# Other places for attention steps, splits and fill matmuls in the periods of a packed-attention and gated-FFN kernel

## The chip, the core and the metric

The kernel runs on one core of a Trainium2 chip. The metric is the device time of one execution in microseconds (us), as the median of the runs. The engines are PE (TensorE: matmuls and transposes), DVE (VectorE), ACT (ScalarE), POOL (GpSimd) and SP (which issues the DMAs).

## The reference, cut to what matters

Eight batches, 8 heads, 576 tokens, head dimension 64, 32 packing queries; then a gated feed-forward layer of 1536 columns over all 4608 tokens. Everything is float32.

```python
def sm_attn(qq, kk, vv):
    s = scale * np.matmul(qq, kk.transpose(0, 1, 3, 2))
    a = np.exp(s - np.max(s, axis=-1, keepdims=True))
    a = a / (np.sum(a, axis=-1, keepdims=True) + 1e-09)
    return np.matmul(a, vv)

p_packed = sm_attn(p, k, v)
x = sm_attn(q, p_packed, p_packed)          # then heads and dims as 512 columns
out = ((x @ w_a) * (x @ w_b)) @ w_out
```

## The kernel before, in words

**The two products of the FFN.** x is never formed. The second attention's weights a2 (transposed, 256 rows by 576 tokens per batch) are multiplied with g = packed values times w_a and w_b. Each float32 factor is split into a rounded part `hi` and a remainder `lo`, and a product is three matmuls: hi·hi, hi·lo, lo·hi. h, the gated product, is split in the same way and multiplied with w_out; this second product is called the fill, since its matmuls (512 columns, L726) are put between those of the first.

**The late part.** Batches 0 and 1 are done by an earlier part of the program. The change and the prediction are about batches 2 to 7, done in 72 periods (`period`, from L816), n = 0 to 71, twelve to a batch; two lead-in periods, -2 and -1, come ahead of them. Period n finishes column block n of h and starts block n + 1, with seven products of 288 columns (`product`, L767):

- products 5 (block n) and 1 (block n + 1) write PSUM bank pair X, product 2 writes V; ACT copies X to `d` (L834);
- first fill; DVE adds V to `d` (L839);
- products 3 and 6 add to X; ACT copies X's half to `c2` (L848); DVE multiplies X by `d` into one half of `hf` (tile name `asb`, L853);
- second fill; products 4 and 7 add to V; DVE adds `c2` to V (L865) and multiplies into the other half of `hf` (L866);
- third fill.

PE must wait where a product writes a bank that another engine still reads: product 3 for the `d` copy, product 4 for the `d` add, product 2 of the next period for the second `hf` multiply. How much PE has to do in between is set by the three fill counts.

**Beside that.** Every second period begins with `make_g` (L781 and after): PE forms g for two blocks, ACT and DVE take it apart, and POOL forms the combinations `gs` (L796). `split_g` (ACT cast `G_hi` at L802, then POOL remainder `G_lo` at L91) and `split_h` (ACT cast `h_hi` at L812, then POOL `h_lo` at L91) make the split factors; `hf` has two buffers. The attention of the batch ahead is cut into steps: `S` and `r` (first attention), `s` (second attention), `L` (loads on SP), `k`, `q`, `T`, `P` (turning of operands), `t` (`half_sums`: four POOL subtractions, L604) and `u0` to `u3` (`half_parts`: ACT casts L618, then remainders on DVE at L91). A u step makes the tiles `a_hi`, `a_lo`, `tx_hi`, `tx_lo` that the next batch's products read.

**What sets the order.** Engines work their queues in the order in which the program is written, and this order is written by hand: the table `STEPS` says which step comes at which point of a period (`pre`, `post`, `a`, `b`, `c`, `end`), one entry for each of the 12 periods of a batch; `FILLS` holds the three fill counts of an even and an odd period, for pairs of periods with 2 and with 3 tiles (24 and 36 matmuls). The places of `split_g` and `split_h` are fixed in `period`: `split_h(n - 1)` ahead of product 3, `split_g` after the `d` copy in odd periods and after the `c2` copy in even ones.

Of the kernel before, what the change touches and what calls it, by code (L numbers as in the profile page):

```python
# [19 lines left out]
def tile_packed_attn_gated_ffn(  # L20
# [483 lines left out]
    SUBS = ("0100")  # L504

    PLAN = (" |  |  | S0 | r0 | r0 |  | r0 |  | r0 Lv1 ; S1 | r1 | r1 q0 Lk2 | r1 | r1 | q1 Lk3 Lv2 P0 |  ; s0 | s0 s0 | s0 T2 | "
            "s0 Lp4 | s0 s1 | s1 s1 | s1 | s1 | s1 | t u0 | k2 |  | k3 Lq2")
    PLAN = dict(enumerate(PLAN.split("|")))
    PLAN_0 = ("A | C C | B A B A | B C C B C | A A | C | B | C B A T0 k0 Lp2 A | A A B B C Lq0 | C C k1 | A B A | "
# [88 lines left out]

    late = {}

    def half_sums(b):

        x0, x1, tf = a2f_of[b, 0], a2f_of[b, 1], late["tf"]
        sub = lambda out, a, c: nc.gpsimd.tensor_tensor(out=out, in0=a, in1=c, op=ALU.subtract)  # L604
        sub(tf[:, 1], x1[:, 1], x0[:, 1])
        sub(x0[:, 1], x0[:, 1], x0[:, 0])
        sub(tf[:, 0], x1[:, 1], x0[:, 1])
        sub(tf[:, 2], x1[:, 0], tf[:, 0])

    def half_parts(b, n):  # L610

# [10 lines left out]
    def emit_steps(b, steps):  # L622

        for name in steps.split():
            if name in "ABCD":
                emit(0, name)
            elif b >= B:
                continue
            elif name == "t":
                half_sums(b)  # L630
# [184 lines left out]
    def period(n, fills, steps):  # L815

        X, V = banks_of["x"], banks_of["v"]
        here, there, more = 0 <= n < LAST, 0 <= n + 1 < LAST, n + 2 < LAST
        k0, k1 = n % 2, (n + 1) % 2
        b = NB + n // NFT  # L820
        both = slice(0 if here and k0 == 0 or there and k1 == 0 else 1, 2 if here and k0 == 1 or there and k1 == 1 else 1)
        step = lambda at: emit_steps(b + 1, steps.get(at, ""))
        step("pre")
        if more and n % 2 == 0:
            make_g(n + 2)
        step("post")
        if here:
            product(n, 5, X, False)
        if there:
            product(n + 1, 1, X, True)  # L830
            product(n + 1, 2, V, True)
        if here or there:
            d = d_of[n] = lp.tile([P, 2, HS], F32, name="d", bufs=2)
            nc.scalar.copy(out=d[:, both], in_=X[:, both, 0:HS])  # L834
        if more and n % 2:
            split_g(n + 2)
        fill(fills[0])
        if here or there:
            nc.vector.tensor_tensor(out=d[:, both], in0=V[:, both, 0:HS], in1=d[:, both], op=ALU.add)  # L839
        flush()  # L840
        step("a")
        split_h(n - 1)
        if here:
            product(n, 3, X, False)
        if there:
            product(n + 1, 6, X, False)
            c2 = c2_of[n + 1] = lp.tile([P, HS], F32, name="c2", bufs=2)
            nc.scalar.copy(out=c2, in_=X[:, k1, 0:HS])  # L848
        if more and n % 2 == 0:
            split_g(n + 2)  # L850
        if here:
            hf = hf_of[n] = sm.tile([P, 2, HS], F32, name="asb")
            nc.vector.tensor_tensor(out=hf[:, 1], in0=X[:, k0, 0:HS], in1=d[:, k0], op=ALU.mult)  # L853
        step("b")
        fill(fills[1])
        flush()
        step("c")
        if here:
            product(n, 4, V, False)
        if there:  # L860
            product(n + 1, 7, V, True)
        if here:
            c2 = c2_of.pop(n)
            v = V[:, k0, 0:HS]
            nc.vector.tensor_tensor(out=v, in0=v, in1=c2, op=ALU.add)  # L865
            nc.vector.tensor_tensor(out=hf[:, 0], in0=v, in1=d_of.pop(n - 1)[:, k0], op=ALU.mult)  # L866
# [13 lines left out]
    while slot[0] <= max(plan) or (slot[0] - start) % 4:  # L880
        fill(6)
        flush()
        between()
    STEPS = {-2: {"post": "u1", "a": "u2", "c": "u3"}, 0: {"pre": "S0", "c": "Lq1", "end": "r0 Lv1"}, 1: {"a": "r0", "b": "r0 r0"},
# [5 lines left out]
    banks_of["x"], banks_of["v"] = bank_pair(), bank_pair()  # L890
    FILLS = {2: ((5, 3, 4), (6, 6, 0)), 3: ((7, 5, 6), (9, 9, 0))}
    for n in (-2, -1):
        period(n, (12, 12, 12), STEPS.get(n, {}))
    fill(99)
    flush()
    for n in range(LAST):
        b, ft = NB + n // NFT, n % NFT
        if ft % 2 == 0:
# [4 lines left out]
        period(n, FILLS[len(some)][ft % 2], STEPS[ft])  # L903
    split_h(LAST - 1)
    fill(99)
    flush()
# [45 lines left out]
```

## Time and profile before

| | |
|---|---|
| median of 3 runs | 718.42 us (718.34 to 718.44) |
| the profiled execution | 717.8 us, span 716.0 us |
| PE busy | 699.4 us, 98% |
| DVE, ACT, POOL busy | 444.8, 360.8, 419.2 us |
| chain that ended last | PE 89%, DVE 4%, POOL 3% |
| DMA | 102.37 MB, mean 143 GB/s |

The span is the time from the first to the last instruction of the profiled execution. A row of a timeline gives start, length, engine, line, operation, out<-in and, in square brackets, idle time of the engine before it and what ended that. Ends of matmuls are modelled, so a PE that waits is read from the starts of its matmuls rather than from its busy share.

### The profile page before, as it was taken

To read this page: it belongs to the slowest core of one execution; us is meant where nothing else is said; L and a number is where in the kernel's file an instruction comes from. 1 tells how busy PE (TensorE), PEld (TensorE's weight loads), DVE (VectorE), ACT (ScalarE), POOL (GpSimd) and SP (SyncE) were. 2 spreads that over 40 slices of the span, in tenths; PEclk is the share of its full clock that TensorE was granted. 3 is DMA by queue.
4 is the path that set the end of the run, shared out by engine and by line. 5 is a ranking of instruction groups with operands and counts; after the bars stand their busy time and mean duration, and the time that the engine had idled before them with its cause. 6 is when DMAs were issued, how large, how long until landed. Compare 5 with 4: busy or idle time off the path is not lost.

```text
span 716.0 us, 14183 instructions
## 1 busy us (share of the span) xinstructions
PE 699.4 (98%) x5558; PEld 574.3 (80%) x5558; DVE 444.8 (62%) x819; ACT 360.8 (50%) x733; POOL 419.2 (59%) x322
## 2 busy tenths in 40 slices
PE   6899999999999999999999999999999999999998
PEld 4488878888878887888888887788788878788887
DVE  3888655467355677665875677665685657654342
ACT  3788744544344555445554456454554445544520
POOL 0595743337245678565875488565776477756520
PEclk9999999999999999999999999999999999999999
DMA  8999863677354725545443563456245323123002
GB/s 256 386 259 307 236 135 72 175 170 272 82 127 149 189 77 149 142 123 148 145 97 122 141 187 92 109 177 165 71 112 165 110 83 119 60 103 133 1 1 74
DMA packets 177059, 102.37 MB, mean 143 GB/s; under 512 B 141280, under 2 KB 159456, under 8 KB 171616
## 3 DMA queue, kind: packets, MB, share of 16 engines
q1 hardware_dynamic: 176992, 101.47, 49.9%
q8 instruction: 43, 0.70, 0.4%
q14 instruction: 24, 0.20, 0.1%
HBM read 85.72 MB, written 15.73 MB: 142 GB/s over the span
## 4 chain that ended last, share of the span: by engine, by line
PE 89%; DVE 4%; POOL 3%; SPq 1%; DMA 1%; ACT 1%; issue 1%; DVEq 0%; POOLq 0%; ACTq 0%
PE x L726 35%; PE m L767 27%; PE m L389 9%; PE m L415 5%; PE x L781 4%; PE s L301 2%; PE s L316 1%; PE s L255 1%; POOL tf L604 1%; PE x L371 1%; DVE tx_lo L91 1%; PE s L291 1%; SPq L116 1%; POOL h_lo L91 1%; DMA kn<-in_k_dram 1%
## 5 line engine op out<-in xcount | busy, mean ns | idle before, releaser
L726 PE MATMUL x<-wo,h_hi 128*128 128x512 f32 (+1 forms) x776 | 242.1, 392 | 0.0
L91 POOL TENSOR_TENSOR h_lo<-asb,h_hi 128x576 fp32r<-128x576 f32 x96 | 139.2, 1450 | 52.5 <-ACT h_hi L408 37.1
L726 PEld LDWEIGHTS x<-wo,h_hi 128*128 128x128 f32 x776 | 138.0, 188 | 20.0 <-ACT gs L787 0.9
L726 PE MATMUL x<-wo,h_lo 128*128 128x512 f32 (+1 forms) x388 | 151.9, 391 | 0.0
L91 POOL TENSOR_TENSOR G_lo<-gs,G_hi 128x640 fp32r<-128x640 f32 x72 | 115.6, 1609 | 53.2 <-ACT G_hi L802 51.1
L91 POOL TENSOR_TENSOR A_lo<-gs,A_hi 128x256 fp32r<-128x256 f32 x36 | 26.8, 744 | 107.0 <-ACT A_hi L790 107.0
L726 PEld LDWEIGHTS x<-wo,h_lo 128*128 128x128 f32 x388 | 72.9, 188 | 13.5
L853 DVE TENSOR_TENSOR asb<-m,d 128x288 f32<-128x288 f32 x72 | 32.7, 455 | 78.0 <-ACT c L848 77.5
L834 ACT COPY d<-m 128x576 f32<-128x576 f32 (+1 forms) x73 | 46.7, 640 | 57.4 <-PE m L767 56.1
L736 DVE TENSOR_TENSOR part<-x,part 128x512 f32<-128x512 f32 (+1 forms) x65 | 44.4, 682 | 37.4 <-PE x L726 37.4
L787 ACT COPY gs<-x 128x512 f32<-128x512 f32 x36 | 21.2, 588 | 89.6 <-PE x L781 89.6
L767 PE MATMUL m<-tx_lo,G_hi 128*128 128x288 f32 x216 | 63.6, 295 | 2.6 <-DVE tx_lo L91 2.6
L839 DVE TENSOR_TENSOR d<-m,d 128x576 f32<-128x576 f32 (+1 forms) x73 | 54.0, 740 | 19.0 <-ACT d L834 18.7
L767 PE MATMUL m<-tx_hi,G_hi 128*128 128x288 f32 x216 | 64.2, 297 | 0.0
L767 PE MATMUL m<-tx_hi,G_lo 128*128 128x288 f32 x216 | 63.7, 295 | 0.0
L802 ACT CAST G_hi<-gs 128x640 fp32r<-128x640 f32 x72 | 52.6, 731 | 14.8 <-POOL gs L796 14.8
L848 ACT COPY c<-m 128x288 f32<-128x288 f32 x72 | 28.9, 402 | 57.4 <-PE m L767 57.4
L767 PEld LDWEIGHTS m<-a_hi,G_hi 128*128 128x128 f32 x144 | 27.0, 187 | 34.6 <-issue 17.4
L812 ACT CAST h_hi<-asb 128x576 fp32r<-128x576 f32 x72 | 49.1, 682 | 5.2 <-DVE asb L866 5.2
L865 DVE TENSOR_TENSOR m<-m,c 128x288 f32<-128x288 f32 x72 | 33.3, 462 | 24.0 <-PE m L767 22.1
L767 PE MATMUL m<-a_hi,G_hi 128*128 128x288 f32 x144 | 46.5, 323 | 1.4 <-ACT d L834 1.4
L796 POOL TENSOR_TENSOR gs<-gs 128x512 f32<-128x512 f32 x36 | 46.8, 1299 | 0.0
(171 smaller groups left out, 1550.7 us busy)
## 6 DMA issues: line engine op xcount, KB each, us to landing
wr<-w_kept SPq DMA_DIRECT2D x36, 1024.0 KB
nat<-in_k_dram SPq DMA_DIRECT2D x56, 144.0 KB
nat<-in_q_dram SPq DMA_DIRECT2D x56, 144.0 KB
vt<-in_v_dram SPq DMA_DIRECT2D x28, 256.0 KB
out_dram<-part SPq DMA_DIRECT2D x27, 256.0 KB
raw<-in_moe_w_a_dram SPq DMA_DIRECT2D x12, 512.0 KB
raw<-in_moe_w_b_dram SPq DMA_DIRECT2D x12, 512.0 KB
raw<-in_moe_w_out_dram SPq DMA_DIRECT2D x12, 512.0 KB
```

The costliest lines, as they stand in the source:

```text
L91: return eng.tensor_tensor(out=dst, in0=src, in1=hi.bitcast(F32), op=ALU.subtract)
L389: nc.tensor.matmul(out=ps[:, half, 0:HS], lhsT=gt[:, kt, ft % 4, cols], rhs=at[:, kt, HS * half:HS * half + HS], start=(n == 0 and kt == 0 ...
L415: nc.tensor.matmul(out=o[:, cols], lhsT=ht[:, c0:c0 + P], rhs=wt[:, cols], start=(ft == 0 and n == 0), stop=(ft == NFT - 1 and n == 2))
L726: nc.tensor.matmul(out=o[:, cols], lhsT=ht[:, c0:c0 + P], rhs=wt[:, cols], start=(ft == fts[0] and n == 0), stop=end)
L736: nc.vector.tensor_tensor(out=parts[i][:, cols], in0=o[:, cols], in1=parts[i][:, cols], op=ALU.add)
L767: nc.tensor.matmul(out=bank[:, n % 2, 0:HS], lhsT=g, rhs=t, start=(first and i == 0), stop=(i == 2), skip_group_check=True)
L796: nc.gpsimd.tensor_tensor(out=gs[:, 2:4].rearrange("p a u f -> p a (u f)"), in0=gs[:, 0:2].rearrange("p a u f -> p a (u f)"), in1=s2.unsqu ...
L802: nc.scalar.copy(out=G_hi[:, n % 3], in_=gs[:, 1:6, n % 2])
L812: nc.scalar.copy(out=view(h_hi[ft]), in_=src)
L834: nc.scalar.copy(out=d[:, both], in_=X[:, both, 0:HS])
L839: nc.vector.tensor_tensor(out=d[:, both], in0=V[:, both, 0:HS], in1=d[:, both], op=ALU.add)
L865: nc.vector.tensor_tensor(out=v, in0=v, in1=c2, op=ALU.add)
```

## The change

Neither the amount of work nor the operations differ. There are more points in a period at which a step can stand (`d`, `v`, `h`, `w`, `f` are new), `split_g` and `split_h` become steps `G` and `H` of the table, `half_sums` is cut into four steps `t0` to `t3`, `STEPS` has 24 entries (12 for the periods of an even batch, 12 for an odd one, beside the two lead-in periods) and `FILLS` a pair of triples for each pair of periods of an even and an odd batch.

```diff
-    def half_sums(b):
+    def half_sum(b, n):
...
+        out, one, two = ((tf[:, 1], x1[:, 1], x0[:, 1]), (x0[:, 1], x0[:, 1], x0[:, 0]),
+                         (tf[:, 0], x1[:, 1], x0[:, 1]), (tf[:, 2], x1[:, 0], tf[:, 0]))[n]
+        nc.gpsimd.tensor_tensor(out=out, in0=one, in1=two, op=ALU.subtract)
...
+                if name == "G":
+                    if more:
+                        split_g(n + 2)
+                elif name == "H":
+                    split_h(n - 1)
...
-        if more and n % 2:
-            split_g(n + 2)
+        step("d")
         fill(fills[0])
         if here or there:
             nc.vector.tensor_tensor(out=d[:, both], in0=V[:, both, 0:HS], in1=d[:, both], op=ALU.add)
+        step("v")
         flush()
         step("a")
-        split_h(n - 1)
...
-        if more and n % 2 == 0:
-            split_g(n + 2)
+        step("h")
...
+        step("w")
...
+        step("f")
...
-             8: {"pre": "s1", "a": "s1", "end": "s1 s1 k2"}, 9: {"a": "s1", "c": "s1", "end": "s1 t"},
-             10: {"a": "u0", "end": "u1"}, 11: {"a": "k3", "c": "u2", "end": "u3 Lq2"}}
+    8: {'pre': 's1', 'post': 's1', 'd': 'H', 'a': 's1', 'c': 'G s1'}, 9: {'pre': 'k2', 'post': 'G', 'd': 's1', 'a': 'H', 'h': 's1', 'f': 's1', 'end': 't0'},
+    10: {'v': 't1 t2 t3', 'a': 'u0', 'b': 'G', 'end': 'H'}, 11: {'post': 'u1', 'v': 'H', 'a': 'k3', 'h': 'Lq2', 'c': 'u2 G', 'f': 'u3'},
...
-    FILLS = {2: ((5, 3, 4), (6, 6, 0)), 3: ((7, 5, 6), (9, 9, 0))}
+    FILLS = [((5, 2, 5), (5, 7, 0)), ((11, 1, 8), (9, 7, 0)), ((5, 0, 5), (6, 8, 0)), ((4, 3, 3), (6, 8, 0)), ((4, 4, 4), (5, 7, 0)), ((6, 3, 3), (7, 5, 0)),
+             ((5, 3, 2), (9, 5, 0)), ((4, 4, 4), (5, 7, 0)), ((5, 4, 4), (6, 5, 0)), ((9, 7, 5), (10, 5, 0)), ((4, 4, 4), (5, 7, 0)), ((9, 4, 7), (8, 8, 0))]
```

(The new tables are broken into lines here; in the code each is one line. The entry `8` here, and `9` to `11`, are those of an even batch.)

The first place is POOL's queue from period 9 to period 10 of batch 2, where batch 3's attention weights become ready. `t1_3148` and `t2_3008` are these weights, `tf_2172` their differences. Before:

```order
L337 TENSOR_TENSOR t1_3057<-t1_3057,sum2_3135 128x576
L604 TENSOR_TENSOR tf_2172<-t1_3148,t2_3008 128x288
L604 TENSOR_TENSOR t2_3008<-t2_3008 128x288
L604 TENSOR_TENSOR tf_2172<-t1_3148,t2_3008 128x288
L604 TENSOR_TENSOR tf_2172<-t1_3148,tf_2172 128x288
L91 TENSOR_TENSOR A_lo_2170<-gs_2171,A_hi_2169 128x256
L796 TENSOR_TENSOR gs_2171<-gs_2171 128x512
```

and after:

```order
L337 TENSOR_TENSOR t1_3039<-t1_3039,sum2_3125 128x576
L606 TENSOR_TENSOR tf_2172<-t1_3148,t2_3008 128x288
L91 TENSOR_TENSOR A_lo_2170<-gs_2171,A_hi_2169 128x256
L794 TENSOR_TENSOR gs_2171<-gs_2171 128x512
L606 TENSOR_TENSOR t2_3008<-t2_3008 128x288
L606 TENSOR_TENSOR tf_2172<-t1_3148,t2_3008 128x288
L606 TENSOR_TENSOR tf_2172<-t1_3148,tf_2172 128x288
```

Three of the four subtractions now stand behind `A_lo` and `gs` instead of ahead of them.

The second place is DVE's queue from period 8 to period 9 of the same batch. `t_3057` before and `t_3039` after are the scores of the second attention. Before:

```order
L91 TENSOR_TENSOR A_lo<-x,A_hi 128x256
L839 TENSOR_TENSOR d<-m,d 128x576
L321 STREAM_TRANSPOSE t_3057<-s 128x576
L853 TENSOR_TENSOR asb<-m,d 128x288
L865 TENSOR_TENSOR m<-m,c_2984 128x288
L866 TENSOR_TENSOR asb<-m,d 128x288
L325 TENSOR_REDUCE mx<-t_3057 128x18
```

and after:

```order
L91 TENSOR_TENSOR A_lo<-x,A_hi 128x256
L321 STREAM_TRANSPOSE t_3039<-s 128x576
L847 TENSOR_TENSOR d<-m,d 128x576
L325 TENSOR_REDUCE mx<-t_3039 128x18
L860 TENSOR_TENSOR asb<-m,d 128x288
L873 TENSOR_TENSOR m<-m,c_2982 128x288
L874 TENSOR_TENSOR asb<-m,d 128x288
```

The transpose has moved ahead of the `d` add, and the maximum ahead of both multiplies.

The third place is PE at the end of period 12, the first of batch 3: the last matmul of product 7, the third fill, and product 5 of period 13. Before:

```order
L767 MATMUL m<-tx_hi,G_lo 128x288
L726 MATMUL x<-wo,h_lo_505 128x512
L726 MATMUL x<-wo,h_hi_506 128x512 x2
L726 MATMUL x<-wo,h_lo_507 128x512
L767 MATMUL m<-a_hi,G_hi 128x288
```

and after:

```order
L765 MATMUL m<-tx_hi,G_lo 128x288
L724 MATMUL x<-wo,h_lo_505 128x512
L724 MATMUL x<-wo,h_hi_506 128x512
L765 MATMUL m<-a_hi,G_hi 128x288
L765 MATMUL m<-a_lo,G_hi 128x288
```

The third fill there has two matmuls instead of four; the other two come later.

More of the change, by code (lines that the diff above doesn't have):

```diff
@@ L506, in tile_packed_attn_gated_ffn @@
     PLAN = (" |  |  | S0 | r0 | r0 |  | r0 |  | r0 Lv1 ; S1 | r1 | r1 q0 Lk2 | r1 | r1 | q1 Lk3 Lv2 P0 |  ; s0 | s0 s0 | s0 T2 | "
-            "s0 Lp4 | s0 s1 | s1 s1 | s1 | s1 | s1 | t u0 | k2 |  | k3 Lq2")
+            "s0 Lp4 | s0 s1 | s1 s1 | s1 | s1 | s1 | t0 t1 t2 t3 u0 | k2 |  | k3 Lq2")
     PLAN = dict(enumerate(PLAN.split("|")))
@@ L628, in emit_steps @@
                 continue
-            elif name == "t":
-                half_sums(b)
+            elif name[0] == "t":
+                half_sum(b, int(name[1]))
             elif name[0] == "u":
@@ L821, in period, with step @@
         both = slice(0 if here and k0 == 0 or there and k1 == 0 else 1, 2 if here and k0 == 1 or there and k1 == 1 else 1)
-        step = lambda at: emit_steps(b + 1, steps.get(at, ""))
+        def step(at):
+            for name in steps.get(at, "").split():
+                if name == "G":
[3 more added lines that the diff above has]
+                    split_h(n - 1)
+                else:
+                    emit_steps(b + 1, name)
         step("pre")
@@ L902, in tile_packed_attn_gated_ffn @@
             filler[0] = mm2_third(part_b, third, some)
-        period(n, FILLS[len(some)][ft % 2], STEPS[ft])
+        period(n, FILLS[n // 2 % NFT][n % 2], STEPS[n % (2 * NFT)])
     split_h(LAST - 1)
```

10 lines of the change are left out of this document (3 added, 7 removed), and 3 rows, old and new, of the table STEPS.

## The prediction, made before the changed kernel ran

> **What bounds the kernel now.** I read the page first, then PE's waits, then the timeline around each wait, engine by engine. From the page:
>
> ```profile
> span 716.0 us, 14183 instructions
> ...
> PE 699.4 (98%) x5558; PEld 574.3 (80%) x5558; DVE 444.8 (62%) x819; ACT 360.8 (50%) x733; POOL 419.2 (59%) x322
> ```
>
> PE is never idle for long, so only what makes PE wait, or its own work, can move the end; the change leaves PE's work as it is. PE's waits, as total, times and longest, have three rows of the late part:
>
> ```profile
> PE m L767 <- DVE tx_lo L91: 2.6, 3, 0.9
> ...
> PE m L767 <- ACT d L834: 1.4, 3, 0.5
> ...
> PE m L767 <- DVE asb L866: 0.3, 1, 0.3
> ```
>
> The first two come three times each, in the same three places; the last, once, near the end. The first, in PE's timeline:
>
> ```profile
> 274.96 0.62 PE L726 MATMUL x<-wo,h_hi 128*128 128x512 f32 x2
> 275.41 0.39 PE L726 MATMUL x<-wo,h_lo 128*128 128x512 f32 x1
> 276.28 0.40 PE L767 MATMUL m<-a_hi,G_hi 128*128 128x288 f32 x1 [0.48 <-ACT d L834]
> ...
> 276.65 0.30 PE L767 MATMUL m<-a_hi,G_lo 128*128 128x288 f32 x1
> 276.78 0.30 PE L767 MATMUL m<-tx_hi,G_hi 128*128 128x288 f32 x1
> 277.93 0.40 PE L767 MATMUL m<-tx_lo,G_hi 128*128 128x288 f32 x1 [0.85 <-DVE tx_lo L91]
> ```
>
> By starts, two fills take 0.45 us (275.41 - 274.96), so one takes 0.23, and a product matmul takes 0.13 (276.78 - 276.65). After the fill at 275.41 the next start came 0.87 later: 0.64 lost. After 276.78 it came 1.15 later: 1.02 lost. Together 1.66 us, in period 11 of batch 2. The bracketed idle times are smaller because ends of matmuls are modelled. The rest of PE's time is pace.
>
> Why it waits stands in the queues of POOL, ACT and DVE:
>
> ```profile
> 268.69 0.81 POOL L604 TENSOR_TENSOR tf<-t,t 128x288 f32<-128x288 f32 x1 [0.89 <-DVE t L341]
> 269.58 0.81 POOL L604 TENSOR_TENSOR t<-t 128x288 f32<-128x288 f32 x1
> 270.48 0.94 POOL L604 TENSOR_TENSOR tf<-t,t 128x288 f32<-128x288 f32 x1
> 271.49 0.91 POOL L604 TENSOR_TENSOR tf<-t,tf 128x288 f32<-128x288 f32 x1
> 272.35 0.74 POOL L91 TENSOR_TENSOR A_lo<-gs,A_hi 128x256 fp32r<-128x256 f32 x1
> 273.05 1.30 POOL L796 TENSOR_TENSOR gs<-gs 128x512 f32<-128x512 f32 x1
> 274.31 1.44 POOL L91 TENSOR_TENSOR h_lo<-asb,h_hi 128x576 fp32r<-128x576 f32 x1
> 275.70 1.55 POOL L91 TENSOR_TENSOR G_lo<-gs,G_hi 128x640 fp32r<-128x640 f32 x1
> ```
>
> ```profile
> 270.84 0.40 ACT L848 COPY c<-m 128x288 f32<-128x288 f32 x1 [0.35 <-PE m L767]
> 274.39 0.73 ACT L802 CAST G_hi<-gs 128x640 fp32r<-128x640 f32 x1 [3.14 <-POOL gs L796]
> 275.02 0.67 ACT L618 CAST tx_hi<-tf 128x576 fp32r<-128x576 f32 x1
> 275.59 0.63 ACT L834 COPY d<-m 128x576 f32<-128x576 f32 x1
> ```
>
> ```profile
> 268.96 0.42 DVE L793 TENSOR_TENSOR gs<-gs,x 128x256 f32<-128x256 f32 x1
> ...
> 270.29 1.43 DVE L91 TENSOR_TENSOR a_lo<-t,a_hi 128x288 fp32r<-128x288 f32 x2
> ...
> 272.83 0.46 DVE L866 TENSOR_TENSOR asb<-m,d 128x288 f32<-128x288 f32 x1
> 273.26 0.69 DVE L736 TENSOR_TENSOR part<-x,part 128x512 f32<-128x512 f32 x1
> 275.79 2.08 DVE L91 TENSOR_TENSOR tx_lo<-tf,tx_hi 128x576 fp32r<-128x576 f32 x1 [1.84 <-POOL h_lo L91]
> ```
>
> The four `t` subtractions, the first released by DVE's transpose, keep POOL until 272.4. `gs`, whose input was ready at 269.38 (L793), ends at 274.35. `G_hi` holds ACT's queue for it 3.14 us, and `tx_hi` and the `d` copy queue behind. `d` ends at 276.22, which is the 0.64; `tx_lo` starts at 275.79, which is the 1.02. The chain of waits shows `gs` at the same point twice more:
>
> ```profile
> 273.09 1.26 POOL gs L796
> ...
> 441.07 1.26 POOL gs L796
> ...
> 608.80 1.26 POOL gs L796
> ```
>
> 168.0 and 167.7 us apart, two batches: the three stalls belong to batches 2, 4 and 6, which have two tiles to fill with in periods 10 and 11. Batches 3 and 5, with three tiles in the same place, show no such wait.
>
> **Term 1, the stalls: 3 x 1.66 = 4.98 us at most.** In the new POOL queue one `t` (0.81) stands ahead of `A_lo` and `gs`, not four. With the lengths above, and with the ends of period 9 where they are: `t0` to 269.50, `A_lo` 269.6 to 270.3, `gs` 270.3 to 271.6, which is 2.75 earlier. `G_hi`, still behind `c2` (ends 271.24), runs 271.6 to 272.3; the 3.14 us wait shrinks to some 0.4. `t1` to `t3` follow `gs`: 271.6 to 274.2, `tx` needing `t2` at 273.4. The cast of `H`, no longer than `G_hi`'s, stands on ACT before `tx_hi`, which runs 273.4 to 274.1, and the `d` copy follows, 274.1 to 274.75. Product 3 of period 11 starts after seven fills instead of six, at 275.41 + 2 x 0.23 = 275.87. It has 1.1 us to spare; the 0.64 goes. What is late next is on DVE.
>
> **Term 2, DVE beside POOL in the same periods: 0 to 0.65 us, three times; taken 0.2.** `tx_lo` took 2.08 us, started 0.09 after `G_lo`, and ended at 277.87, 0.62 after `G_lo` did (277.25). The two `a_lo` took 1.43 together beside `t` subtractions; the later single ones are shorter:
>
> ```profile
> 280.70 0.43 DVE L91 TENSOR_TENSOR a_lo<-t,a_hi 128x288 fp32r<-128x288 f32 x1
> ```
>
> So these remainders wait while POOL works, and the new plan puts the longer `gs` (1.30) where a `t` was. The first `a_lo` is due at 270.29. If it starts ahead of `gs`, nothing changes: 0. If `gs` is ahead, the first `a_lo` ends at 271.6 + 0.35, the second behind `t1` at about 273.05, 1.3 later than now; the three DVE operations behind them (0.46 each by L866's row) end near 274.45. Product 2 of period 11 waits for the last of these:
>
> ```profile
> 273.86 0.30 PE L767 MATMUL m<-a_hi,A_hi 128*128 128x288 f32 x1
> ```
>
> That would cost some 0.65. Between the ends: in the new order the transpose that releases `t0` comes a few tenths earlier, because its sums stand ahead of both multiplies; then `gs` ends near 271.05, the second `a_lo` near 272.5, the last multiply near 274.0, and PE loses some 0.2. I take that, nearer the lower end. `tx_lo` then waits for `G_lo` as today, and ends near 276.4, just when product 6 asks for it (275.87 + 0.40 + 0.13 = 276.40): nothing more on top of the shift. Three times 0.2 is 0.6 us.
>
> The Trainium skill, SBUF — State Buffer, Who interferes with whom, says that a DVE instruction with two SBUF inputs and a GpSimd instruction that reads SBUF lock each other out, the first holding the port for its whole length. The trace agrees (the 0.62 above), and by that rule the upper end of this term would be the likelier one, 0.65 each; it has its own rival below.
>
> **Term 3, thinner covers elsewhere (periods counted 0 to 23 over an even and an odd batch): 0, bounds 0 and 0.3 us at eleven places.** Where the third fill of period 12 drops from four to two (batches 3, 5, 7), product 2 starts 0.46 us earlier against the multiply ahead of it:
>
> ```profile
> 287.52 0.46 DVE L866 TENSOR_TENSOR asb<-m,d 128x288 f32<-128x288 f32 x1
> ...
> 288.56 0.30 PE L767 MATMUL m<-a_hi,A_hi 128*128 128x288 f32 x1
> ```
>
> 288.56 - 287.98 = 0.58 to spare, 0.12 afterwards. Where the transpose is put ahead of the `d` add (periods 8 and 20, five times), this add ends 0.66 later (one start to the next):
>
> ```profile
> 257.24 0.75 DVE L839 TENSOR_TENSOR d<-m,d 128x576 f32<-128x576 f32 x1
> 257.90 0.77 DVE L321 STREAM_TRANSPOSE t<-s 128x576 f32<-128x576 f32 x1
> 258.94 0.46 DVE L853 TENSOR_TENSOR asb<-m,d 128x288 f32<-128x288 f32 x1 [0.26 <-ACT c L848]
> ...
> 259.00 0.30 PE L767 MATMUL m<-tx_hi,G_hi 128*128 128x288 f32 x1
> ```
>
> Product 4 starts 1.01 after it; 0.35 stays. Period 4 (three times) loses its second fill, 3 x 0.23 = 0.69: out of the same 1.01, 0.32 stays. All are covered, by little. Every other step stays covered: the weight and operand loads move by one or two points, `Lv2` ahead of one weight load on SP, and each has most of a period before its reader. Fewer than zero is not to be had: PE does not wait there now.
>
> **The sum.** Span 716.0 - 4.98 + 0.6 = 711.6. Outside the span lie 1.8 us (717.8 - 716.0), which the change does not touch: 713.4 for a profiled execution. The median of the runs stands 0.62 above the profiled one: 714.0 us.
>
> **The rivals.**
>
> - *DVE and POOL lock each other out at the worse order.* This is term 2 at its upper end: 0.65 at product 2 and up to 0.3 at product 6's `tx_lo`, say 0.8, in three places: 718.42 - 4.98 + 2.4 = 715.8. For it: `a_lo` is due within 0.1 us of `gs`. Against: the earlier release of `t0`.
> - *The stall only moves: no change.* Besides that, the eleven thin covers are overrun by 0.3 each, 3.3 us: 718.42 - 4.98 + 2.4 + 3.3 = 719.1. For it: covers of 0.12 to 0.35 against durations that vary by 0.6 where DVE meets POOL. Against: the DVE operations at these places have one input in PSUM, and their lengths in the rows above hardly vary.
> - *Slower, through the two `hf` buffers.* `H` now stands at the end of periods 5, 10, 12 and 19 (twelve times in all), so `h_lo(n - 1)` reaches POOL up to a period later, and the first multiply of period n + 1 (L853) may not overwrite `hf` before it ends. In an even period that multiply starts 3.90 us after product 5:
>
> ```profile
> 255.04 0.40 PE L767 MATMUL m<-a_hi,G_hi 128*128 128x288 f32 x1
> ```
>
> With `h_lo` at 1.45, POOL may be 2.4 us behind when the period starts. PE itself must wait only from product 1 of the next period, nine product matmuls and four fills after 259.00, at 261.1; the multiply (258.94 to 259.40) may slip 1.7 until then. From 4.1 us of backlog on, each further 0.1 counts twelve times; at 5.0 it is 12 x 0.9 = 10.8, and 718.42 - 4.98 + 10.8 = 724.2. Against it: POOL is busy 59% of the time, and `h_lo` stands ahead of the next `A_lo` at these points, except behind three `t` and a `G_lo` in period 10.
>
> That the change does not do what it says is excluded: the queues' order shows it.
>
> **How the numbers follow.** The forecast, 714.0, has 0.62, with a range of its own from 712.9 (no term 2: 713.4; the last wait of 0.3 gone too, and 0.2 of scatter) to 714.8. The lock-out rival has 0.20, no change 0.12, the `hf` rival 0.06. A measurement of this kernel tells about 0.2%, 1.4 us, from no change. Both first cases are faster by more: 0.82, cut to 0.80 for the tail of the second; no change gives 0.13, slower 0.07. The range from 712.9 to 717.0 holds the first case and the second with its margin, and leaves out some 0.2.
>
> **What would show it.** In the profile after: no PE wait for `ACT d`; `G_hi`'s wait for `gs` at period 10 from 3.14 to under 0.6; `gs` ends near 271.5 and the two-batch spacing shrinks from 168.0 to about 166.5; at product 2 of period 11 a wait of 0 to 0.65 for L874. Wrong would be new waits of PE for DVE's L847 or L874 in periods 4, 8, 12 or 20, or for L860 behind POOL's `h_lo`, or the old waits where they were.

## The result, and the profile after

The changed kernel takes 714.75 us (median of 4 runs, 714.0 to 715.27), the kernel before beside it 718.43 us (718.34 to 718.98, 4 runs). The ratio is 0.9946, with a 95% interval from 0.9929 to 0.9964: faster, by some 3.7 us. The forecast was 714.0, with a range from 712.9 to 717.0.

From the page of the kernel after:

```profile
span 712.2 us, 14198 instructions
...
PE 699.0 (98%) x5558; PEld 574.2 (81%) x5558; DVE 449.8 (63%) x819; ACT 363.2 (51%) x733; POOL 417.8 (59%) x322
...
PE 94%; DVE 2%; SPq 1%; DMA 1%; ACT 1%; issue 0%; DVEq 0%; ACTq 0%
```

PE does the same work in 3.8 us less span, and POOL has left the chain that ended last. DVE is busy 5.0 us longer with the same 819 instructions: some of them got slower, which will matter below. In the list of PE's waits only one row of the late part is left (total, times, longest), the single one near the end; those for `d` and `tx_lo`, three times each, are gone:

```profile
PE m L765 <- DVE asb L874: 0.3, 1, 0.3
```

Lines have moved: products are now L765, fills L724, the `d` copy L843, the `d` add L847, the two multiplies into `hf` L860 and L874, `G_hi` L800, `gs` on POOL L794, `t` L606. The queues around the old stall, at the end of batch 2, POOL first:

```profile
268.90 0.81 POOL L606 TENSOR_TENSOR tf<-t,t 128x288 f32<-128x288 f32 x1 [1.17 <-DVE t L341]
269.67 0.74 POOL L91 TENSOR_TENSOR A_lo<-gs,A_hi 128x256 fp32r<-128x256 f32 x1
270.37 1.30 POOL L794 TENSOR_TENSOR gs<-gs 128x512 f32<-128x512 f32 x1
271.62 1.02 POOL L606 TENSOR_TENSOR t<-t 128x288 f32<-128x288 f32 x1
...
276.01 3.38 POOL L91 TENSOR_TENSOR h_lo<-asb,h_hi 128x576 fp32r<-128x576 f32 x2
279.34 1.55 POOL L91 TENSOR_TENSOR G_lo<-gs,G_hi 128x640 fp32r<-128x640 f32 x1
```

One `t` stands ahead of `A_lo` and `gs`, and `gs` ends at 271.67 (it was 274.35). Counted from product 5 of period 10, which starts 0.71 us later in this profile (268.09 against 267.38), that is 3.58 us instead of 6.97. ACT now does not wait for it:

```profile
272.07 0.73 ACT L800 CAST G_hi<-gs 128x640 fp32r<-128x640 f32 x1
272.70 0.68 ACT L810 CAST h_hi<-asb 128x576 fp32r<-128x576 f32 x1
273.66 0.68 ACT L616 CAST tx_hi<-tf 128x576 fp32r<-128x576 f32 x1 [0.28 <-POOL tf L606]
274.74 0.64 ACT L843 COPY d<-m 128x576 f32<-128x576 f32 x1 [0.41 <-PE m L765]
```

The idle time of 3.14 us ahead of `G_hi` has no bracket any more; the `d` copy waits for PE instead of PE for it. DVE in the same stretch, and on into the next period:

```profile
270.94 2.02 DVE L91 TENSOR_TENSOR a_lo<-t,a_hi 128x288 fp32r<-128x288 f32 x2
...
273.76 0.46 DVE L874 TENSOR_TENSOR asb<-m,d 128x288 f32<-128x288 f32 x1
...
274.73 1.93 DVE L91 TENSOR_TENSOR tx_lo<-tf,tx_hi 128x576 fp32r<-128x576 f32 x1
276.58 0.74 DVE L847 TENSOR_TENSOR d<-m,d 128x576 f32<-128x576 f32 x1
277.25 1.36 DVE L124 STREAM_TRANSPOSE xT<-nat 128x1152 f32<-128x1152 f32 x1
278.54 0.41 DVE L860 TENSOR_TENSOR asb<-m,d 128x288 f32<-128x288 f32 x1
278.88 0.67 DVE L734 TENSOR_TENSOR part<-x,part 128x512 f32<-128x512 f32 x1
279.48 1.73 DVE L91 TENSOR_TENSOR a_lo<-t,a_hi 128x288 fp32r<-128x288 f32 x1
...
281.62 0.46 DVE L874 TENSOR_TENSOR asb<-m,d 128x288 f32<-128x288 f32 x1
```

The `a_lo` at 279.48 (step u2) is the new late comer. It took 0.43 us in the kernel before (280.70 there) and takes 1.73 here; it ends at 281.21. PE in period 12, where product 5 is the first to read it:

```profile
280.88 0.40 PE L765 MATMUL m<-a_hi,G_hi 128*128 128x288 f32 x1
281.26 0.40 PE L765 MATMUL m<-a_lo,G_hi 128*128 128x288 f32 x1
...
281.90 0.29 PE L765 MATMUL m<-a_hi,A_lo 128*128 128x288 f32 x1
282.13 0.40 PE L765 MATMUL m<-a_hi,A_hi 128*128 128x288 f32 x1
```

Product matmuls follow each other by 0.13 us, the first one behind `make_g` by 0.24 (282.07 to 282.31 in the kernel before). Here the second one starts 0.38 after the first, at 281.26, which is 0.05 after the end of `a_lo`; product 2 (282.13) starts 0.05 after L874 ends at 282.08. The list of waits shows neither, since modelled ends cover so short a gap: they have to be read from starts.

**A measure free of the early part.** From product 5 of period 0 to product 5 of period 70, before and then after:

```profile
198.53 0.40 PE L767 MATMUL m<-a_hi,G_hi 128*128 128x288 f32 x1
...
680.74 0.30 PE L767 MATMUL m<-a_hi,G_hi 128*128 128x288 f32 x1
```

```profile
199.24 0.40 PE L765 MATMUL m<-a_hi,G_hi 128*128 128x288 f32 x1
...
676.98 0.30 PE L765 MATMUL m<-a_hi,G_hi 128*128 128x288 f32 x1
```

This "late part" is 482.2 us before and 477.7 after: 4.5 us gained. The start of it comes 0.7 us later in the profile after, and that is why the spans differ by 3.8 only. The change is not the reason: the lead-in periods are the only work ahead of it that it touches, and from their first `make_g` to product 5 of period 0 both kernels take 21.93 us. Period lengths below are from one product 5 to the next. Period 11 of batch 2 fell from 9.01 to 7.13 us, and it recurs in batches 4 (9.01 to 7.13) and 6 (8.57 to 6.68): 5.65 us came from there. Period 12, the first of the next batch, has fewer fills under the new plan and should have shrunk to 5.2; it takes 5.71 (the same in period 36, and 5.42 in period 60).

### The profile page after: what moved, and what is told of

Its sections match the earlier page's. It is cut to its first block, busy times and chain, and to the rows that moved or that the text cites. A ratio compares the mean times of both kernels' runs of the same rounds, so it can differ in the third digit from the quotient of the medians.

```text
span 712.2 us, 14198 instructions
## 1 busy us (share of the span) xinstructions
PE 699.0 (98%) x5558; PEld 574.2 (81%) x5558; DVE 449.8 (63%) x819; ACT 363.2 (51%) x733; POOL 417.8 (59%) x322
## 4 chain that ended last, share of the span: by engine, by line
PE 94%; DVE 2%; SPq 1%; DMA 1%; ACT 1%; issue 0%; DVEq 0%; ACTq 0%
PE x L724 37%; PE m L765 29%; PE m L389 9%; PE x L779 5%; PE m L415 5%; PE s L301 2%; PE s L316 1%; PE s L255 1%; PE x L371 1%; PE s L291 1%; SPq L116 1%; DMA kn<-in_k_dram 1%; DMA nat<-in_k_dram 0%; PE m L152 0%; PE x L152 0%
## 5 line engine op out<-in xcount | busy, mean ns | idle before, releaser
L724 PE MATMUL x<-wo,h_hi 128*128 128x512 f32 (+1 forms) x776 | 249.3, 391 | 0.0
L724 PEld LDWEIGHTS x<-wo,h_hi 128*128 128x128 f32 x776 | 140.8, 188 | 22.2 <-ACT gs L785 1.0
L724 PE MATMUL x<-wo,h_lo 128*128 128x512 f32 (+1 forms) x388 | 152.1, 392 | 0.0
L91 POOL TENSOR_TENSOR G_lo<-gs,G_hi 128x640 fp32r<-128x640 f32 x72 | 113.0, 1575 | 30.6 <-ACT G_hi L800 30.3
L724 PEld LDWEIGHTS x<-wo,h_lo 128*128 128x128 f32 x388 | 72.9, 188 | 11.8
L847 DVE TENSOR_TENSOR d<-m,d 128x576 f32<-128x576 f32 (+1 forms) x73 | 54.0, 740 | 34.6 <-ACT d L843 33.8
L860 DVE TENSOR_TENSOR asb<-m,d 128x288 f32<-128x288 f32 x72 | 32.4, 451 | 66.4 <-ACT c L856 64.8
L765 PE MATMUL m<-tx_hi,G_hi 128*128 128x288 f32 x216 | 63.8, 296 | 0.0
L765 PE MATMUL m<-tx_hi,G_lo 128*128 128x288 f32 x216 | 63.7, 295 | 0.0
L765 PE MATMUL m<-tx_lo,G_hi 128*128 128x288 f32 x216 | 63.3, 293 | 0.0
L800 ACT CAST G_hi<-gs 128x640 fp32r<-128x640 f32 x72 | 52.2, 730 | 15.1 <-POOL gs L794 14.5
L843 ACT COPY d<-m 128x576 f32<-128x576 f32 (+1 forms) x73 | 46.6, 639 | 20.2 <-PE m L765 18.6
L765 PEld LDWEIGHTS m<-a_hi,G_hi 128*128 128x128 f32 x144 | 27.0, 187 | 31.6 <-issue 17.4
L794 POOL TENSOR_TENSOR gs<-gs 128x512 f32<-128x512 f32 x36 | 46.7, 1296 | 2.6 <-DVE gs L791 2.5
L765 PE MATMUL m<-a_hi,G_hi 128*128 128x288 f32 x144 | 47.0, 326 | 0.0
L389 PE MATMUL m<-a_hi,ghi 128*128 128x288 f32 x192 | 43.2, 307 | 1.5 <-ACT ghi L377 1.5
```

What stands on the lines that cost most here:

```text
L91: return eng.tensor_tensor(out=dst, in0=src, in1=hi.bitcast(F32), op=ALU.subtract)
L389: nc.tensor.matmul(out=ps[:, half, 0:HS], lhsT=gt[:, kt, ft % 4, cols], rhs=at[:, kt, HS * half:HS * half + HS], start=(n == 0 and kt == 0 ...
L724: nc.tensor.matmul(out=o[:, cols], lhsT=ht[:, c0:c0 + P], rhs=wt[:, cols], start=(ft == fts[0] and n == 0), stop=end)
L765: nc.tensor.matmul(out=bank[:, n % 2, 0:HS], lhsT=g, rhs=t, start=(first and i == 0), stop=(i == 2), skip_group_check=True)
L794: nc.gpsimd.tensor_tensor(out=gs[:, 2:4].rearrange("p a u f -> p a (u f)"), in0=gs[:, 0:2].rearrange("p a u f -> p a (u f)"), in1=s2.unsqu ...
L800: nc.scalar.copy(out=G_hi[:, n % 3], in_=gs[:, 1:6, n % 2])
```

## The experiments

Every kernel was run beside the kernel before. "Period 11" and "period 12" are those at the end of batch 2 and the start of batch 3; without a wait period 11 takes 7.13, and period 12 5.68 with the old fill counts and 5.2 with the new.

| kernel | late part | period 11 | period 12 | median (range) | ratio to before, 95% |
|---|---|---|---|---|---|
| before | 482.20 | 9.01 | 5.68 | | |
| after | 477.73 | 7.13 | 5.71 | 714.75 (714.0-715.27) | 0.9946 (0.9929-0.9964) |
| after, once more | 477.75 | 7.13 | 5.70 | 715.22 (715.13-715.3) | 0.9939 (0.9921-0.9958) |
| t split only | 481.47 | 8.63 | 5.68 | 717.96 (717.17-719.78) | 0.9989 (0.998-0.9997) |
| after, t together | 480.50 | 7.86 | 5.93 | 716.97 (716.42-717.78) | 0.9972 (0.9961-0.9983) |
| after, old fills | 478.49 | 7.14 | 6.16 | 714.9 (713.95-717.59) | 0.9948 (0.9933-0.9963) |
| t and h | 478.88 | 7.49 | 6.15 | 715.89 (715.59-717.22) | 0.9955 (0.994-0.997) |
| t, h and s1, first form | 480.84 | 7.15 | 5.68 | 717.3 (716.5-718.11) | 0.9975 (0.9965-0.9985) |
| t, h and s1, second form | 478.93 | 7.47 | 6.15 | 715.49 (715.22-716.37) | 0.9952 (0.9939-0.9966) |
| t, h and s1, third form | 477.43 | 7.14 | 6.07 | 713.67 (713.5-714.6) | 0.9932 (0.9918-0.9945) |
| after, u2 first | 478.10 | 7.82 | 5.22 | 714.98 (713.36-715.41) | 0.9938 (0.9926-0.995) |
| after, G late | 478.37 | 7.13 | 5.66 | 714.78 (714.64-714.99) | 0.9934 (0.992-0.9947) |
| after, u2 first, S0 later | 479.08 | 8.30 | 5.21 | 715.77 (714.98-717.23) | 0.995 (0.9935-0.9965) |
| after, k3 early, u2 first | 476.77 | 7.13 | 5.21 | 713.06 (712.82-713.91) | 0.9915 (0.9902-0.9929) |

### What varies by itself: the kernel after once more

> The kernel after once more, unchanged. If the part ahead of product 5 of period 0 is what varies between executions and the rest is fixed by the order of work, the late part is 477.7 us again within 0.1, while product 5 of period 0 starts anywhere from 198.5 to 201.3 us. Rival: the late part varies too, by 0.3 us or more, and differences of that size between the experiments mean nothing.

The late part came out at 477.75 us (477.73 the first time), its start at 199.50 (199.24). Over all the executions here the start lies anywhere from 198.5 to 201.2 us, although from the first `make_g` of the lead-in periods on all kernels take the same 21.9 us to it: what varies lies ahead of that. So, as far as one repeat shows, differences of 0.1 us in the late part mean something, and medians, with their spread of 1 to 2 us, are the coarser measure.

### One part alone: the t split

The kernel before, with `half_sums` cut up and nothing else:

```diff
-  9: {"a": "s1", "c": "s1", "end": "s1 t"},  10: {"a": "u0", "end": "u1"},
+  9: {"a": "s1", "c": "s1", "end": "s1 t0"}, 10: {"a": "t1 t2 t3 u0", "end": "u1"},
```

> The kernel before with one edit: half_sums is cut into four steps, t0 stays at the end of period 9, t1 to t3 stand after the d add of period 10. Theory (the three stalls come from the three subtractions ahead of gs, nothing else is needed): the waits of product 3 and product 6 in period 11 go, 1.86 us each in three places by the starts of the matmuls, so 718.4 - 5.6 = 712.8; some of it may be given back to DVE's remainders beside POOL, up to 1.3, so 712.8 to 714.1. Rival (the new places of G and H and the fills are needed as well): G_hi or the remainders stall PE anyway, 716.5 or more.

It gained 0.7 us of the 4.5. The rows for `d` and `tx_lo` are gone from PE's waits, but there is a new one:

```profile
PE m L765 <- POOL G_lo L91: 3.0, 3, 1.0
```

POOL's queue, then PE's product 6, show the place:

```profile
276.99 1.43 POOL L91 TENSOR_TENSOR h_lo<-asb,h_hi 128x576 fp32r<-128x576 f32 x1
278.39 3.59 POOL L91 TENSOR_TENSOR G_lo<-gs,G_hi 128x640 fp32r<-128x640 f32 x2
```

```profile
279.19 0.31 PE L765 MATMUL m<-tx_lo,G_hi 128*128 128x288 f32 x1
280.50 0.40 PE L765 MATMUL m<-tx_hi,G_lo 128*128 128x288 f32 x1 [1.01 <-POOL G_lo L91]
```

`t1` to `t3` no longer stand ahead of `gs`, but they and `h_lo` stand ahead of the `G_lo` that product 6 reads. PE loses 1.18 us by starts (280.50 - 279.19 - 0.13). My prediction took it that moving the `t` off `gs` removes the stalls; done alone it hands most of them to the next one in POOL's queue. The median is the rival's, through `G_lo`, which the rival had not named.

### All but that part: the plan after, with t together

```diff
-  9: {..., 'end': 't0'},  10: {'v': 't1 t2 t3', 'a': 'u0', ...}
+  9: {..., 'end': 't0 t1 t2 t3'},  10: {'a': 'u0', ...}
```

> The kernel after with t0 to t3 together at the end of period 9 in even batches, all else of the new plan kept. Theory: gs ends 2.7 us later again, G_hi waits about 3 us for it, PE loses about 1.9 us three times: 714.7 + 4.5 to 5.7, so 719 to 720.5. Rival (the new plan without the moved subtractions covers them): 714.7 to 715.5.

The late part lost 2.8 of the 4.5 us. The wait for `d` returned (1.3 us in three), but period 11 took 7.86, not 9.01: the rest of the plan alone takes 1.1 us off each stall, and the median of 716.97 lies between my two cases. Neither half gives the whole: 0.7 for the split alone, 1.7 for all the rest, 4.5 for both.

### The fill counts

The kernel after with the old triples in every pair of periods:

```diff
-    FILLS = [((5, 2, 5), (5, 7, 0)), ((11, 1, 8), (9, 7, 0)), ...]
+    FILLS = [((5, 3, 4), (6, 6, 0)), ((7, 5, 6), (9, 9, 0)), ...]
```

> The kernel after with the fill counts of before in every pair of periods. Theory: the fill counts carry nearly none of the gain, since the covers of before were enough: 714.2 to 715.2. Rival (half of the gain is in the fills): 716.5.

The late part grew by 0.76 us, of which 0.63 lie in periods 60 and 61 (13.26 together against 12.63). There the matmul of product 5 that reads u2's `a_lo` starts 0.79 us after the first instead of 0.24. With the old fills `a_lo` and POOL's `G_lo` start at the same 611.65:

```profile
611.65 1.86 DVE L91 TENSOR_TENSOR a_lo<-t,a_hi 128x288 fp32r<-128x288 f32 x1
...
611.65 1.55 POOL L91 TENSOR_TENSOR G_lo<-gs,G_hi 128x640 fp32r<-128x640 f32 x1
```

In the kernel after, `a_lo` is 0.03 ahead:

```profile
612.19 0.45 DVE L91 TENSOR_TENSOR a_lo<-t,a_hi 128x288 fp32r<-128x288 f32 x1
...
612.22 1.83 POOL L91 TENSOR_TENSOR G_lo<-gs,G_hi 128x640 fp32r<-128x640 f32 x1
```

One of the two goes through at its own length and the other is stretched; some hundredths of a microsecond settle which, and most of this run's loss hangs on that. In period 12 it waits as without the edit (6.16 against 5.68: 0.48). The fills moved to other places carry a sixth of the gain at most, and 0.13 us without periods 60 and 61.

### Two moves

The t split, and the split of h behind that of G in period 10; nothing else changed from before:

```diff
-        split_h(n - 1)
+        if n % NFT != 10:
+            split_h(n - 1)
...
         fill(fills[2])
         flush()
+        if n % NFT == 10:
+            split_h(n - 1)
         step("end")
```

> The kernel before with two moves and no other: t0 at the end of period 9 and t1, t2, t3 early in period 10 (as in the run with the t split alone), and the split of h moved to the end of period 10, behind the split of G. In the t split alone GpSimd's order t1 t2 t3 h_lo G_lo made G_lo late and TensorE waited 1.2 us per pair at product 6; with h_lo behind G_lo this wait should go. Theory (two moves carry the gain of the whole change): the late part, product 5 of period 0 to product 5 of period 70, is 476.6 to 478.0 us (before 482.2, after 477.7), the time 712.8 to 715.0, no TensorE wait for d or G_lo above 0.3 us. Rival (the other moved steps are needed as well): a wait stays in periods 11 and 12, late part 479.5 or more, time 716.5 or more.

478.88 us lies between the two: the G_lo wait is gone as forecast, and 3.3 of the 4.5 us are there, but a rest stays: 0.36 us in period 11, 0.12 in period 10. Period 12 waits here too (6.15 against 5.68): u2's `a_lo` starts at 280.73, 0.02 after an `h_lo` of 1.42 us, and takes 1.71. So the two moves alone bring this wait; it does not come from the new places of the other steps. Compared at the same point (times from product 5 of period 0), `gs` ends 72.9 us after it here and 72.4 in the kernel after:

```profile
271.62 1.29 POOL L794 TENSOR_TENSOR gs<-gs 128x512 f32<-128x512 f32 x1
```

(272.91 - 199.99; in the kernel after 271.67 - 199.24.) POOL's `t0` starts 0.5 later as well, released by the last transpose of the softmax: some of the softmax steps s1 must come sooner.

### A third move, in three forms

The first form, in even batches, on top of the two moves:

```diff
+    8: {"pre": "s1", "post": "s1", "a": "s1", "c": "s1"},
+    9: {"pre": "k2", "a": "s1", "b": "s1", "c": "s1", "end": "t0"}
```

> The kernel with the two moves (t split, split of h behind that of G in period 10), and one more: the steps s1 of the softmax in periods 8 and 9 of even batches one place earlier, about as in the kernel after. With the two moves alone the late part was 478.88 us against 477.73 of the kernel after: the last transpose of the softmax ended 0.5 us later, t0 and gs behind it, and TensorE still waited 0.36 us in period 11 and 0.12 in period 10 per pair. Theory (the head start of the softmax steps is the third part of the gain): the late part falls to 477.4 to 477.9 us, period 11 to 7.13 us. Rival (another of the many moved steps is behind the rest): 478.5 or more.

It backfired. DVE's transpose, which must wait for POOL's division, now stood ahead of V's add and multiply, and PE's product 2 waited for these in period 10:

```profile
270.61 0.40 PE L765 MATMUL m<-a_hi,A_hi 128*128 128x288 f32 x1 [1.08 <-DVE asb L865]
```

Periods 11 and 12 then ran free (7.15 and 5.68), but as PE had come 1.3 us later, this says nothing for the theory.

The second form:

```diff
-    9: {"pre": "k2", "a": "s1", "b": "s1", "c": "s1", "end": "t0"}
+    9: {"pre": "k2", "a": "s1", "b": "s1", "end": "s1 t0"}
```

> The last run moved the softmax steps so that the final transpose of the softmax stood ahead of V's addition and product in period 9, and these then waited for GpSimd's division: TensorE waited 1.2 us in period 10 for the product. Here the final step of s1 is back at the end of period 9, as in the two-move kernel, and only the step with the sum and the reciprocal is one place earlier, so that GpSimd's division is done when the transpose is asked for. Theory (the two-move kernel lacks only this head start of about 0.5 us for t0 and gs): no wait in period 10, period 11 at 7.13 us as in the kernel after, late part 477.2 to 477.7 us against 478.88, the time 713.8 to 715.2. Rival (the rest of the plan carries what is missing): late part 478.5 or more.

It moved nothing that counts: between the points `b` and `c` DVE is given nothing else there, so the sum stayed where it was in its queue, the reciprocal starting 67.76 us after product 5 of period 0 in both kernels. It measured the two-move kernel again (478.93), and tells nothing apart. The third form:

```diff
+        step("h")
         if here:
             hf = hf_of[n] = sm.tile([P, 2, HS], F32, name="asb")
...
-    9: {"pre": "k2", "a": "s1", "b": "s1", "end": "s1 t0"}
+    9: {"pre": "k2", "a": "s1", "h": "s1", "end": "s1 t0"}
```

> The last run left VectorE's order as it was: the sum and the reciprocal still stood behind the product into the first half of h, and began at the same point of the pair as in the two-move kernel. Here they stand ahead of it, as in the kernel after, so GpSimd's division can start about 1 us sooner. Theory (the two-move kernel lacks only the head start of the softmax): t0 and gs come 0.4 to 0.5 us sooner, period 11 falls from 7.49 to 7.1 to 7.2 us and period 10 from 5.79 to 5.68, the wait of period 12 stays (6.15), late part 477.2 to 477.8 us, time 713.8 to 715.2. Rival (other moved steps carry what is missing): late part 478.5 or more.

It puts sum and reciprocal ahead of the multiply into the first half of `hf`, as the change does. DVE's row of the reciprocal, and POOL's of `gs`:

```profile
266.36 0.27 DVE L336 RECIPROCAL sum<-sum 128x18 f32<-128x18 f32 x1
```

```profile
270.27 1.29 POOL L794 TENSOR_TENSOR gs<-gs 128x512 f32<-128x512 f32 x1
```

From product 5 of period 0 (199.13) the reciprocal starts at 67.23 instead of 67.76, `gs` ends at 72.43, as in the kernel after, and the waits of periods 10 and 11 are gone. The late part is 477.43 us. So three moves around periods 8 to 10 are enough for the whole gain of the change: t split, split of h behind G in period 10, sums of the softmax ahead of a multiply. On top of these the other moved steps and fills are worth nothing together (477.73 with them).

### The wait of period 12: u2 first

The step u2 ahead of k3 (the transpose into `xT`) in period 11 of the kernel after:

```diff
-  11: {'post': 'u1', 'v': 'H', 'a': 'k3', 'h': 'Lq2', 'c': 'u2 G', 'f': 'u3'}
+  11: {'post': 'u1', 'v': 'H', 'a': 'u2 k3', 'h': 'Lq2', 'c': 'G', 'f': 'u3'}
```

> The kernel after with step u2 moved ahead of k3 in period 11 of even batches (from point c to point a). Theory: the new wait at product 5 of period 12 comes from u2's remainder a_lo, which stands on DVE behind k3's transpose (1.36 us) and is locked out by G_lo (1.73 instead of 0.45 us); earlier, it ends before it is asked for, and the waits at products 5 and 2 of period 12 go: 0.5 us for two batches and about 0.25 for the third, so 714.7 - 1.3 = 713.4. Rival (period 12's third fill of two is too thin whatever u2 does): 714.7 as it is, with the wait at product 2 left.

The wait of period 12 went (5.71 to 5.22), and period 11 grew by 0.69. DVE's rows and PE's:

```profile
278.09 1.02 DVE L91 TENSOR_TENSOR a_lo<-t,a_hi 128x288 fp32r<-128x288 f32 x1
279.04 1.36 DVE L124 STREAM_TRANSPOSE xT<-nat 128x1152 f32<-128x1152 f32 x1
```

```profile
280.20 0.96 PE L255 MATMUL s<-xT,pT 64*32 64x288 f32 x16
...
282.39 0.41 PE L765 MATMUL m<-a_hi,G_hi 128*128 128x288 f32 x1
```

`xT` ends at 280.40, after the 16 small matmuls that read it have begun; with `make_g` behind them they take 2.19 us to product 5, in the kernel after 1.50 (279.38 to 280.88). The wait moved from `a_lo` to `xT`.

### Shut out, or only late? G behind u3

```diff
-  11: {..., 'c': 'u2 G', 'f': 'u3'}
+  11: {..., 'c': 'u2', 'f': 'u3', 'end': 'G'}
```

> The kernel after with one step moved: the split of G of period 11 goes from its third place in the period to the end, behind u3, so that GpSimd's G_lo and h_lo subtractions no longer lie beside VectorE's a_lo of u2. Theory (two-SBUF-input instructions of the two engines shut each other out): that a_lo falls from 1.73 to about 0.5 us, TensorE's wait for it at product 5 of period 12 goes (0.4 to 0.5 us per pair), late part 476.5 to 477.3 us unless the later G_lo or G_hi brings a wait of its own at product 1 or 4 of period 12. Rival (a_lo is late because it is queued behind xT and the part addition, not because it is shut out): a_lo stays at 1.2 us or more or starts as late, the wait stays within 0.15 us of the 0.5, late part 477.5 to 478.

"Shut out" means that an instruction has started but gets on only when the other engine's is done. DVE's two `a_lo` and POOL's `G_lo`:

```profile
279.72 0.43 DVE L91 TENSOR_TENSOR a_lo<-t,a_hi 128x288 fp32r<-128x288 f32 x1
...
280.95 1.46 DVE L91 TENSOR_TENSOR a_lo<-t,a_hi 128x288 fp32r<-128x288 f32 x1
```

```profile
280.52 1.56 POOL L91 TENSOR_TENSOR G_lo<-gs,G_hi 128x640 fp32r<-128x640 f32 x1 [0.91 <-ACT G_hi L800]
```

With POOL idle beside it, u2's `a_lo` takes 0.43 us, and the next one, now beside `G_lo`, 1.46, ending 0.33 after `G_lo` (282.41 against 282.08). In the kernel after the 1.73 us ended 0.32 after `G_lo` (281.21 against 280.89). The lengthening follows POOL's instruction and not the place in DVE's queue: the shut-out is shown. The wait for `a_lo` is gone, but `gs`'s copy on ACT now starts behind `G_lo`, PE's fill waits 0.35 + 0.10 for it, and period 12 is as long as before the edit (5.66). In period 60 the fill waits longer for the same copy (6.11 against 5.42), and so the late part is 478.37 us, above the ranges of both my cases.

### S0 behind make_g

```diff
-  11: {..., 'a': 'k3', ..., 'c': 'u2 G', ...},    12: {'pre': 'S0', ...}
+  11: {..., 'a': 'u2 k3', ..., 'c': 'G', ...},    12: {'post': 'S0', ...}
```

> The kernel after with u2 ahead of k3 in period 11 (as in the run before) and, new, the 16 small matmuls and the make_g that need k3's xT put behind the products of period 12 instead of ahead of them. Theory (the wait only moved from a_lo to xT, and there is a place that waits for neither): late part 476.5 to 477.0 us, about 0.7 to 1.2 us under after, time about 713.7. Rival (the new place has a price of its own: make_g's result is late for the fill or the split of period 13, or the switch to the small matmuls costs the same again): late part 477.7 or more.

The place is not what my expectation says: `post` stands behind `make_g` and still ahead of product 5. The rival's loss came, by another way than it named:

```profile
279.51 1.83 PE L779 MATMUL x<-wr,ppT 64*32 64x512 f32 x12
280.77 0.69 PE L255 MATMUL s<-xT,pT 64*32 64x288 f32 x8
281.16 0.61 PE L779 MATMUL x<-wr,ppT 64*32 64x512 f32 x4
```

Eight of `make_g`'s matmuls ran at once, the second eight began at 280.70, and product 5 came 2.67 us after the start instead of 1.50. DVE's addition into `part`, behind `xT` in its queue, ended at 280.65; as PSUM banks are handed out in turn, I take it that the second half of `make_g` got the bank which that addition still read. That was not tested.

### k3 two periods earlier

```diff
-   9: {..., 'd': 's1', 'a': 'H', ...},            11: {..., 'a': 'k3', ..., 'c': 'u2 G', 'f': 'u3'}
+   9: {..., 'd': 's1', 'v': 'k3', 'a': 'H', ...}, 11: {..., 'a': 'u2', ..., 'c': 'G', 'f': 'u3'}
```

> The kernel after with two steps of even batches moved: k3 (the 1.36 us transpose of k) from period 11 to period 9, behind the addition into d, where VectorE stood idle for 1.05 us; and u2 into the place in period 11 that k3 left. With u2 first alone the wait of period 12 went (84.95 to 84.46 us per 12 periods) but the small matmuls that read k3's result waited in its place (81.64 to 82.29). Theory (both waits come from k3 and u2 standing in one queue in one period): neither is left, the late part is 476.4 to 476.9 us, the time about 713.3 to 714.0. Rival (VectorE has no room: k3 now makes the softmax steps late, and t0, gs and tx_lo behind them): a wait of 0.3 us or more at product 6 of period 11, late part 477.5 or more.

Both waits are gone. DVE has the transpose where it stood idle, and `a_lo` ends 2.8 us before it is read:

```profile
264.92 1.37 DVE L124 STREAM_TRANSPOSE xT<-nat 128x1152 f32<-128x1152 f32 x1
266.21 0.72 DVE L334 TENSOR_REDUCE m<-t 128x18 f32<-128x576 f32 x1
...
278.10 1.02 DVE L91 TENSOR_TENSOR a_lo<-t,a_hi 128x288 fp32r<-128x288 f32 x1
```

```profile
281.72 0.40 PE L765 MATMUL m<-a_hi,G_hi 128*128 128x288 f32 x1
281.96 0.30 PE L765 MATMUL m<-a_lo,G_hi 128*128 128x288 f32 x1
```

The late part is 476.77 us, 0.96 under the kernel after, as forecast, and the median of 713.06 (712.82 to 713.91) is a little under the 713.3 to 714.0 that I gave it and below all runs of the kernel after. Against before it is the best of all: 0.9915 (0.9902 to 0.9929). The 0.96 is most of what the change gave back in period 12: 0.50 is won back in each of batches 3 and 5. Batch 7 stays nearly as it was (period 60 takes 5.38, in the kernel after 5.42, where 5.21 is free): `a_lo` is not late there, but the copy of `gs` on ACT stands behind `G_lo` (it starts at 614.09 in the kernel after, `G_lo` ending at 614.05), and PE's first fill waits for it.

## Why the prediction was right, point by point

**What bounds the kernel: right.** With PE's work unchanged, the gain is PE's waits, in the three places named.

**Term 1: the mechanism right, the size too small.** `gs` ends 3.58 us after product 5 of period 10 (forecast 3.67 in the middle case), the two-batch spacing is 166.6 and 166.3 (forecast about 166.5), `G_hi` does not wait, `d` and `tx_hi` are on time, all three stalls are gone. But each cost 1.88 us (9.01 - 7.13), not 1.66, so 5.65 in all instead of 4.98. The starts show the rest: in the kernel before the matmul behind each of the two waits was followed after 0.24 us instead of 0.13 (276.28 to 276.65 is 0.37 for two), so 0.64 + 0.11 + 1.02 + 0.10 is 1.87. I had counted the two gaps and not what follows them. That the t split is what removes the stalls is right only together with the split of h behind G and the earlier sums: the split alone brought 0.7 us.

**Term 2: the mechanism right, the place wrong, the size about half.** The first `a_lo` did come behind `gs` (it ended at 271.98, 0.31 after it), the order that I had called the worse one. But t0 and `gs` came sooner, as in the middle case that I took (its 3.67 is 271.05 - 267.38). L874 ended at 274.22, and product 2 of period 11 started 0.32 later. The loss that I put there at 0.2 is 0. It arose one period later, at u2's `a_lo`, which stands behind `xT` and `part` and is then shut out by `G_lo` (279.34 to 280.89): 0.50 us each in periods 12 and 36, and 0.21 in period 60, where `G_lo` is the one stretched, by the lengths against a free 5.21. That is 1.21 us in all, where the term had 0.6. That batch 7 paid 0.21 and not more is luck: `a_lo` was 0.03 ahead of `G_lo` there, and with the old fills, where it was not, period 60 lost 0.88 (6.56 against 5.68). The step that failed is the search for the next late thing: it stopped at `tx_lo`, and the row quoted for a later remainder, 0.43 us at 280.70, was taken for the length that it would keep.

The Trainium skill, SBUF — State Buffer, Who interferes with whom, says that a DVE instruction with two SBUF inputs contends with a GpSimd instruction that reads SBUF. The trace agrees, with a length for it: 0.43 us free, 1.46 to 1.86 beside `G_lo`.

**Term 3: right, with one of my signs against it.** The covers were as thin as worked out, and held: the spare time at product 2 behind period 12 is 0.09 to 0.11 us (forecast 0.12), at a price of 0.05 there (287.39 to 287.57 instead of 0.13 on), at product 4 of periods 8 and 20 0.34 (0.35), of period 4 0.31 (0.32). Moved fills are worth little either way. But a new wait for L874 in period 12, which I had named as a sign of being wrong, did come: product 2 starts 0.05 after L874 there and loses 0.2 us with the gap behind it. It is part of the 0.50 of term 2 and not a cover that was too thin: L874 is late because it stands behind the late `a_lo`.

**The sum: two errors that cancel.** Forecast -4.98 + 0.6 = -4.38; measured in the late part -4.47, made of -5.65, +1.21 and -0.03 over the other periods. Term 1 was 0.67 too small and term 2 0.61: that the sum came out within 0.1 is luck. That the median moved by 3.7 and not 4.5 lies within the scatter of the early part; the repeat of the kernel after stood 4.3 under before (715.22 against 719.5).

**The rivals.** The no-change rival needed the eleven thin covers to be overrun: none was. The rival through the two `hf` buffers cost PE nothing: DVE's L860 does wait for `h_lo` once, 0.7 us in period 59, but PE has no wait there and the period takes the free 6.68. The lock-out rival was right on the order of `a_lo` and `gs` and wrong on its price, since `gs` came sooner than it supposed. The one that was near, and that I had not named, is the stall handed to `G_lo`: the order of G and H in the new table is what averts it.

## What to carry to other kernels

When a stall is removed by taking work out of one engine's queue, follow that work to its new place and ask who queues behind it there: the t split alone handed 1.2 of 1.9 us on to `G_lo`, and only the order of three steps together gave the whole gain. Where two engines shut each other out, an operation's length belongs to its neighbour: price it by the other engine's instruction beside it, at its new place, not by its own row at the old one. And compare such kernels over a stretch of the trace that starts behind whatever varies by itself: 0.3 us could be told in the late part where medians spread over more than 1 us.

## What the runs showed of the hardware that I had not expected

- A product matmul that PE starts after a wait is followed 0.24 us later instead of 0.13, so a wait costs about 0.10 us beyond its own length. The same 0.10 is seen at 281.72 in the kernel with k3 early, at the first product matmul behind `make_g`, where I see nothing that it waits for.
- Shut out, a remainder of 288 columns ends about 0.33 us after POOL's instruction does (0.32 and 0.33 above), most of its free length of 0.43: it does next to nothing of its work beside it. When it starts first, even by 0.03 us (612.19 against 612.22), it keeps its own length, 0.45, and POOL's `G_lo` takes 1.83 instead of 1.55.
- The early part of the program, the same in kernels that differ only in late periods, ends anywhere in a range of 2.7 us (198.53 in the kernel before, 201.24 in the t split alone). Some of its waits are for loads, as this row of the t split alone shows, which the kernels before and after do not have:

```profile
PE s L301 <- DMA vt<-in_v_dram: 1.7, 2, 1.4
```
